# Items of 224 rows, and the start and tail of the work on other queues, in a sigmoid attention with top-1 experts

## The chip, the cores and the metric

The kernel runs on one core of a Trainium2 chip. A core has TensorE (PE, with a separate weight-load stream, PEld), VectorE (DVE), ScalarE (ACT), GpSimd (POOL) and SyncE (SP), and 16 DMA engines that serve the queues into which SP, ACT and POOL issue their transfers. The metric is the device time of one execution in microseconds, as the median of several runs.

## The reference

Attention without softmax for 8 batches, 12 heads, 448 rows and heads of 64, and then for each of the 3584 tokens the one expert of eight that a gate chooses:

```python
def _attn_ref(q, k, v):
    S = q.shape[2]
    scale = 1.0 / np.sqrt(q.shape[-1])
    scores = scale * np.matmul(q, k.transpose(0, 1, 3, 2)) - np.log(S)
    attn = 1.0 / (1.0 + np.exp(-scores))
    return np.matmul(attn, v)

def _moe_ref(x, w_gate, w1, w2):          # x: 3584 x 768
    logits = x @ w_gate                   # 8 experts
    expert_idx = np.argmax(logits, axis=1)
    ...                                   # gate_w: the chosen expert's softmax weight
    for e in range(E):
        mask = expert_idx == e
        h = np.maximum(x[mask] @ w1[e], 0.0)      # 768 -> 1024
        out[mask] = gate_w[mask, None] * (h @ w2[e])   # 1024 -> 768
    return out
```

Everything is float32.

## The kernel before

**Attention.** Two heads make a pair (48 pairs), two pairs a unit (24 units), and a unit takes 7 steps, one for each 64 of the 448 key rows; 168 steps in all. A step makes the scores of two pairs (L541, PE), takes the sigmoid of each (L528, ACT: two activations a step, `at`) and multiplies by the values (L555, PE), which are added up over the 7 steps in PSUM. In the first units the products with the values run two steps behind the scores. The scores have four PSUM buffers, which is two steps: the scores of step 6 are written where those of step 4 stood, after ACT has read them. The order on each engine is the order in which the instructions are written.

For a pair g, k and q are loaded in four DMAs each (`kn`, `qn`, L458; called kg and qg here: k4 is k of pair 4), turned by DVE (L512, `kt`, `qt`), and the values are loaded as `vn`: one DMA for an even pair (L466), two for an odd one (L504). Pairs 0 and 1 are loaded in natural order (`first`, on SP and ACT) and turned by PE. k goes on SP's queue, q on SP's, or on POOL's for pairs 3, 7, 9 and 11. The values of pair 0 go on ACT's queue, those of the pairs up to 15 on POOL's. Within a unit, `READY` says after which step the next loads and turns are written.

SP's and ACT's DMAs share a ring of eight completion counters, called DMAHW0 to DMAHW7 in the order listing, POOL's DMAs have DMASW0 to DMASW7. A DMA that takes a counter in use waits on the issuing engine until the DMA before it on that counter has landed.

**Experts.** When a unit's sums are complete, they are split into a high half (`xh`, L563, a cast on ACT) and a low half (`xl`, L564, DVE), and three products stand for one float32 product. For each batch, all 448 tokens go through the expert that most of them chose (L220 and L239), in between the attention steps from step 36 on. The tokens that chose another expert are recorded in a table in DRAM, `recs`, which is first filled with blank records (L112 to L117), and are computed anew at the end.

**The left-over rows.** At the end the records are cut into items of TL = 256 rows of one expert. A full item goes through `Item.run`: it gathers its rows in two tiles of 128, turns them (L808), multiplies by w1 (stage 1, L869: 144 matmuls with a moving side of TL columns) and by w2 (stage 2, L889: 144 with a stationary side of 128 rows and a moving side of 256 columns), and scatters the two tiles into the output (L818, POOL). An item of at most 32 rows goes another way (`few_first`, `few_turn`, `few_rows`), whose last products run behind the full item's (L929), are scaled by DVE (L933), and are scattered by POOL (L934). With the inputs that are timed there are 218 left-over rows of one expert and one row of another, so one item is full and one has few rows, before the change and after it. A helper, `apart`, tells the framework that two scatters write different rows, so that the second needn't wait for the first; before the change the two scatters of one item are told apart, and those of the few rows are not told apart from them.

Of the kernel before, what the change touches and what calls it, by code (L numbers as in the profile page):

```python
# [19 lines left out]
P = 128  # L20
# [5 lines left out]
def tile_sigmoid_attention_top1_moe(  # L26
# [85 lines left out]
    def blank_records():  # L112
        blank = wpool.tile([P, 1024], U32, tag="wst", bufs=RAWS_AHEAD, name="blank")
        blank3 = blank[:, : E * NT // P * 2].rearrange("p (r w) -> p r w", w=2)
        for w, val in enumerate((int(BIG), 0)):
            nc.gpsimd.iota(blank3[:, :, w], pattern=[[0, E * NT // P]], base=val, channel_multiplier=0)
        nc.gpsimd.dma_start(recs.rearrange("(p r) w -> p r w", p=P), blank3)  # L117
# [376 lines left out]
    def load_values(g):  # L494
        if g >= NG:
            return
        b, hp = divmod(g, NP)
        eng = nc.scalar if g == 0 else nc.gpsimd if g < V_POOL else nc.sync
        t = apool.tile([P, KC, D], F32, tag="vn", bufs=4, name=f"vn_{g}")
        if g % 2 == 0:  # L500
            both_heads(t.rearrange("p c d -> p (c d)"), v, g, eng)
        else:
            for h in range(2):
                eng.dma_start(t[quarter(g, h)], v[b, 2 * hp + h].rearrange("(p c) d -> p c d", c=KC))  # L504
        ops[g, "v"] = t
# [39 lines left out]
    def weighted(s):  # L545
        u, c = divmod(s, ST)
        two = [2 * u + n for n in range(2)]
        for g in two:
            if c == 0:
                pool, tag = (ps_av, "av") if u % 2 == 0 or s >= ALONE else (ps_moe, "moe")  # L550
                psv[g] = pool.tile([P, 512], F32, tag=tag, name=f"av_{g}")
            at = ats.pop((g, c))
            for h in range(2):
                rows = quarter(g, h)
                nc.tensor.matmul(  # L555
                    psv[g][OWN[h], :S], ops[g, "v"][rows, c, :], at[rows], start=(c == 0), stop=(c == KC - 1)
                )
        if c == KC - 1:
            for g in two:
                pv = psv.pop(g)  # L560
                xh = xpool.tile([P, S], F32R, tag="xh", name=f"xh_{g}")
                xl = xpool.tile([P, S], F32R, tag="xl", name=f"xl_{g}")
                nc.scalar.copy(xh, pv[:, :S])  # L563
                nc.vector.tensor_sub(xl, pv[:, :S], xh.bitcast(F32))  # L564
                token_block(g, pv[:, :S])
                xch[divmod(g, NP)] = (xh, xl)

    WARM, V_POOL = 32, 16
# [14 lines left out]
    def attention():  # L583
# [13 lines left out]
        for g in (2, 3):  # L597
            load_values(g)
        blank_records()
# [20 lines left out]
        for s in range(N_ST + 11):  # L620
# [5 lines left out]
            if s < ALONE:  # L626
                steps(s, 1, s - 1)
            elif s == ALONE:
                steps(s, 1, s)
            elif i == ST - 1:  # L630
                steps(s - ST + 2, ST, s + 1)
            yield s, MIX[0]
# [56 lines left out]
    TL = 2 * P  # L689
# [57 lines left out]
    li = rest.tile([1, TL], I32, name="li")  # L747
    nc.vector.tensor_copy(li, pli[0:1, :TL])
    more(8)

    recs_v = recs.rearrange("(i t p) w -> i p t w", t=2, p=P)
    recs_f = recs.rearrange("(i t p) w -> i t p w", t=TL // FEW, p=FEW)
    rec_c = rest.tile([P, 2, 2], U32, name="rec_c")
    rec_n = rest.tile([P, 2, 2], U32, name="rec_n")
# [18 lines left out]
    def load_raw(st, ereg, r):  # L773

        if r < 6:
            f, tp = divmod(r, 3)
            src = w1[bass.ds(ereg, 1), tp * TL : (tp + 1) * TL, f * 512 : (f + 1) * 512]
            nc.sync.dma_start(raw_view(st, 512), src.rearrange("e (t p) f -> p (e t) f", p=P))
        else:
            w2_rows(ereg, r - 6, st)  # L780

    def get_rows(ireg, rec):
        nc.sync.dma_start(rec, recs_v[bass.ds(ireg, 1)].rearrange("o p t w -> (o p) t w"))
        for t in range(2):
            nc.gpsimd.indirect_dma_start(
                out=xg[:, t, :],
                out_offset=None,
                in_=x_tok,
                in_offset=bass.IndirectOffsetOnAxis(ap=rec[:, t, 0:1], axis=0),
                bounds_check=NT - 1,  # L790
                oob_is_err=False,
            )
# [6 lines left out]
    def sort_rows():  # L799
        for t in range(2):  # L800
            sorted_row(xp[:, t], xg[:, t])

    def split_rows(k2):
        px = ps_x.tile([P, 512], F32, tag="px", name=f"px_{k2}")
        for kk in range(2):
            for t in range(2):
                at = kk * TL + t * P
                nc.tensor.transpose(px[:, at : at + P], xp[:, t, 2 * k2 + kk], ident)  # L808
# [6 lines left out]
    def scatter(rec):  # L815
        puts = []
        for t in range(2):
# [3 lines left out]
                in_=xo[:, t, :],  # L821
# [4 lines left out]
            apart(put, puts)  # L826

    pairs, h_two = [], []

    class Item:  # L830
# [23 lines left out]
        def run(self, rec):  # L854
# [25 lines left out]
            for d in range(ND):  # L880
                pss = [ps_m2.tile([P, 512], F32, tag="m2", name=f"ps2_{d}_{h}")[:, :DW] for h in range(2)]
                for n in range(4):
                    whi, wlo = self.part(u)
                    for h in range(2):
                        for i in range(2):
                            hh, hl = (x[:, h * P : (h + 1) * P] for x in hts[2 * n + i])
# [8 lines left out]
                for h in range(2):  # L895
                    to, gate = xo[:, h, d * DW : (d + 1) * DW], rec[:, h, 1:2].bitcast(F32)
# [4 lines left out]
            scatter(rec)  # L901
# [21 lines left out]
    def few_rows():  # L923
# [10 lines left out]
        nc.gpsimd.indirect_dma_start(  # L934
# [6 lines left out]
        )  # L941

# [31 lines left out]
    for t in range(2):  # L974
        nc.gpsimd.indirect_dma_start(
            out=xg[:, t, :],
# [48 lines left out]
    with tc.If(n_items >= 2), tc.manual_schedule():  # L1025
        one.run(rec_c)
    for r in range(9, NR):
        last_raw(r)
    with tc.If(n_few >= 1), tc.manual_schedule():
        few_rows()  # L1030
# [47 lines left out]
```

## Time and profile before

| | |
|---|---|
| median of 3 runs | 824.16 us (823.64 to 824.49) |
| the profiled execution's own time | 823.56 us |
| its span, first to last instruction | 821.5 us |
| PE busy | 810.7 us, 99% |
| DVE, ACT, POOL busy | 398.9, 382.5, 142.9 us |
| mean granted TensorE clock | 0.997 |
| first attention step's scores | 7.8 us after the start |
| stage 1, stage 2 of the full item | 774.8 to 792.0, 792.0 to 809.3 us |
| DMA traffic | 120.68 MB, 147 GB/s |

The lines that the prediction shows come from the page of this execution and from answers of its trace. A row of a timeline has the start and the length in us, the engine, the source line, the operation, its tiles (out<-in) and how many instructions are taken together; in brackets stand the time that the engine sat idle before it and what ended that. SPq, ACTq and POOLq are the queues on which DMAs are issued. A row of the chain that ended last has the start, the length and what it was.

### The profile page before, as it was taken

The page shows a single profiled execution, that of the slowest core. Times are in us where ns is not written, and L with a number is a line of the kernel's source. Part 1 is how long each engine was busy: PE and PEld are TensorE (multiplying, and loading weights), DVE is VectorE, ACT ScalarE, POOL GpSimd, SP SyncE. Part 2 cuts the span into 40 slices and gives each one's busy share as a digit, 9 for nine tenths or more (in the row PEclk, how much of TensorE's full clock was granted, in tenths as well). Part 3 has the DMA queues.
Part 4 walks back from the last instruction along what each step waited for, and adds up shares of the span by engine and source line. Part 5 has one row for each costly group of instructions (what it writes and reads, how often), then busy time and mean ns, then how long its engine had stood idle before and what let it go on. Part 6 is the DMA issues. An engine that isn't in the chain of part 4 may idle for free.

```text
span 821.5 us, 15350 instructions
## 1 busy us (share of the span) xinstructions
PE 810.7 (99%) x5712; PEld 618.2 (75%) x5712; DVE 398.9 (49%) x852; ACT 382.5 (47%) x672; POOL 142.9 (17%) x213
## 2 busy tenths in 40 slices
PE   8999999999999999999999999999999999999995
PEld 5547678677687686786786876876867868999894
DVE  2466346345473264453562544733654435755461
ACT  5865634444525535436344445255362452233250
POOL 4444003110041001310031100410015001512201
PEclk9999999999999999999999999999999999999998
DMA  9999865493485663953847855647635422757840
GB/s 170 162 174 192 216 148 125 108 228 90 116 184 107 163 152 84 204 139 98 184 94 135 203 117 117 165 93 181 127 101 144 127 71 55 204 175 246 273 165 36
DMA packets 287104, 120.68 MB, mean 147 GB/s; under 512 B 200258, under 2 KB 278997, under 8 KB 287024
## 3 DMA queue, kind: packets, MB, share of 16 engines
q1 hardware_dynamic: 277712, 98.81, 51.5%
q0 software_dynamic: 8880, 20.14, 10.3%
q8 instruction: 47, 0.77, 0.4%
q10 hardware_dynamic: 432, 0.69, 0.2%
q14 instruction: 33, 0.27, 0.1%
HBM read 97.55 MB, written 23.17 MB: 147 GB/s over the span
## 4 chain that ended last, share of the span: by engine, by line
PE 98%; DMA 0%; POOL 0%; issue 0%; POOLq 0%; ACT 0%; ACTq 0%
PE ps L239 29%; PE ps L220 29%; PE sc L541 16%; PE av L555 16%; PE psg L267 2%; PE ps L889 2%; PE ps L869 2%; DMA out_dram<-xo,rec_c 0%; PE ps_warm L519 0%; PE pl L276 0%; PE few L912 0%; PE sc_first_k L483 0%; PE sc_first_q L483 0%; PE px L808 0%; PE pg L392 0%
## 5 line engine op out<-in xcount | busy, mean ns | idle before, releaser
L528 ACT ACTIVATE at<-sc,bias_s 128x448 f32<-128x448 f32 x336 | 195.9, 632 | 133.8 <-PE sc L541 132.8
L541 PE MATMUL sc<-qt,kt 64*64 64x448 f32 x1344 | 173.5, 544 | 0.9 <-ACT at L528 0.9
L555 PE MATMUL av<-at,vn 64*64 64x448 f32 x1344 | 172.0, 537 | 0.0
L255 POOL DMA_DIRECT2D out_dram<-ob x96 | 61.4, 651 | 465.7 <-DVE ob L250 387.4
L239 PE MATMUL ps<-hh,w2l 128*128 128x448 f32 x384 | 142.0, 370 | 0.0
L239 PE MATMUL ps<-hh,w2h 128*128 128x448 f32 x384 | 141.6, 369 | 0.0
L220 PE MATMUL ps<-xl,w1h 128*128 128x448 f32 x384 | 141.3, 368 | 0.0
L239 PE MATMUL ps<-hl,w2h 128*128 128x448 f32 x384 | 141.0, 367 | 0.0
L220 PE MATMUL ps<-xh,w1l 128*128 128x448 f32 x384 | 140.6, 366 | 0.0
L220 PE MATMUL ps<-xh,w1h 128*128 128x448 f32 x384 | 140.4, 366 | 0.0
L564 DVE TENSOR_TENSOR xl<-av,xh 128x448 fp32r<-128x448 f32 x48 | 29.1, 605 | 219.8 <-ACT xh L563 217.6
L541 PEld LDWEIGHTS sc<-qt,kt 64*64 64x64 f32 x1344 | 77.4, 189 | 61.6 <-issue 28.1
L225 ACT ACTIVATE hh<-ps 128x448 fp32r<-128x448 f32 x64 | 34.9, 545 | 159.3 <-PE ps L220 159.2
L555 PEld LDWEIGHTS av<-at,vn 64*64 64x64 f32 x1344 | 63.4, 132 | 60.2 <-issue 26.0
L145 ACT CAST w2h<-wst 128x512 fp32r<-128x512 f32 x96 | 61.6, 659 | 86.9 <-PE ps L239 75.3
L220 PEld LDWEIGHTS ps<-xl,w1h 128*128 128x128 f32 x384 | 72.1, 188 | 10.8 <-issue 5.2
L239 PEld LDWEIGHTS ps<-hh,w2h 128*128 128x128 f32 x384 | 72.2, 188 | 9.4 <-issue 4.2
L239 PEld LDWEIGHTS ps<-hh,w2l 128*128 128x128 f32 x384 | 72.2, 188 | 8.3 <-issue 2.8
L220 PEld LDWEIGHTS ps<-xh,w1l 128*128 128x128 f32 x384 | 72.1, 188 | 7.8 <-issue 1.4
L220 PEld LDWEIGHTS ps<-xh,w1h 128*128 128x128 f32 x384 | 72.1, 188 | 6.5 <-issue 0.7
L239 PEld LDWEIGHTS ps<-hl,w2h 128*128 128x128 f32 x384 | 72.2, 188 | 6.0 <-issue 0.4
L146 DVE TENSOR_TENSOR w2l<-wst,w2h 128x512 fp32r<-128x512 f32 x96 | 64.0, 683 | 22.5 <-ACT w2h L145 20.0
(166 smaller groups left out, 737.1 us busy)
## 6 DMA issues: line engine op xcount, KB each, us to landing
wst<-in_moe_w_dram SPq DMA_DIRECT2D x48, 512.0 KB
wst<-in_moe_w_dram SPq DMA_DIRECT2D x56, 384.0 KB
x_tok<-xt SPq DMA_DIRECT2D x64, 168.0 KB
out_dram<-ob POOLq DMA_DIRECT2D x96, 112.0 KB
kn<-in_k_dram SPq DMA_DIRECT2D x184, 56.0 KB
qn<-in_q_dram SPq DMA_DIRECT2D x168, 56.0 KB
raw<-in_moe_w_dram SPq DMA_DIRECT2D x12, 512.0 KB
kept<-in_moe_w_dram SPq DMA_DIRECT2D x12, 512.0 KB
```

The costliest lines, as they stand in the source:

```text
L145: nc.scalar.copy(hi, st)
L146: eng.tensor_tensor(lo, st, hi.bitcast(F32), op=ALU.subtract)
L220: nc.tensor.matmul(ps[:, :S], a[:, ws], b_, start=(t == 0 and n == 0), stop=(t == KD - 1 and n == 2))
L225: nc.scalar.activation(hh[:, :S], ps[:, :S], AF.Relu)
L239: nc.tensor.matmul(ps[:, :S], a, b_, start=(j == 0 and n == 0), stop=(j == KF - 1 and n == 2))
L255: nc.gpsimd.dma_start(out[b * S : (b + 1) * S, cols].rearrange("(j r) f -> r j f", r=32), obv[32 * i : 32 * (i + 1)])
L267: nc.tensor.matmul(psg[: 2 * E, :S], wgs[:, t], xch[b, t][n], start=(t == 0 and n == 0), stop=(t == KD - 1 and n == 1),)
L528: nc.scalar.activation(at, ps[:, :S], AF.Sigmoid, bias=bias_s, scale=SCALE)
L541: nc.tensor.matmul(ps[quarter(g, h), :S], ks, ops[g, "q"][OWN[h]], start=True, stop=True)
L555: nc.tensor.matmul(psv[g][OWN[h], :S], ops[g, "v"][rows, c, :], at[rows], start=(c == 0), stop=(c == KC - 1))
L564: nc.vector.tensor_sub(xl, pv[:, :S], xh.bitcast(F32))
L869: nc.tensor.matmul(pss[j], a[:, js], b_, start=(t == 0 and m == 0), stop=(t == KD - 1 and m == 2))
```

## The change

1. An item has 224 rows in two tiles of 112 (`RT = S // 4`, `TL = 2 * RT`). Stage 1 moves 224 columns, stage 2 has a stationary side of 112, gathers, scatters and transposes have 112 rows, and the tables over the possible items have 128 entries for 112.
2. The scatter of the few rows is told apart from the two of the full item.
3. The values of pairs 2 and 3 are loaded on ACT's queue, after steps 2 and 3 are written, where POOL issued them at the start. The blank records are made where they were, and written by SP after step 12.
4. For units that end before step 35 (five units, ten casts) DVE makes the high half, where ACT did.

```diff
     def blank_records():
         ...
-        nc.gpsimd.dma_start(recs.rearrange("(p r) w -> p r w", p=P), blank3)
+        return lambda: nc.sync.dma_start(recs.rearrange("(p r) w -> p r w", p=P), blank3)
...
     def load_values(g):
...
-        eng = nc.scalar if g == 0 else nc.gpsimd if g < V_POOL else nc.sync
+        eng = nc.scalar if g in V_ACT else nc.gpsimd if g < V_POOL else nc.sync
...
-                nc.scalar.copy(xh, pv[:, :S])
+                if s < ALONE:
+                    nc.vector.tensor_copy(xh, pv[:, :S])
+                else:
+                    nc.scalar.copy(xh, pv[:, :S])
...
-    WARM, V_POOL = 32, 16
+    WARM, V_POOL, V_ACT = 32, 16, (0, 2, 3)
...
-        for g in (2, 3):
-            load_values(g)
-        blank_records()
+        write_blank = blank_records()
         gate_halves()
...
+            if s in (2, 3):
+                load_values(s)
+            elif s == 2 * ST - 2:
+                write_blank()
             yield s, MIX[0]
...
-    TL = 2 * P
+    RT = S // 4
+    TL = 2 * RT
...
     def split_rows(k2):
...
-                at = kk * TL + t * P
-                nc.tensor.transpose(px[:, at : at + P], xp[:, t, 2 * k2 + kk], ident)
+                at = kk * TL + t * RT
+                nc.tensor.transpose(px[:, at : at + RT], xp[:RT, t, 2 * k2 + kk], ident[:RT, :RT])
...
     def scatter(rec):
...
-                in_=xo[:, t, :],
+                in_=xo[:RT, t, :],
...
             apart(put, puts)
+        return puts
...
-                            hh, hl = (x[:, h * P : (h + 1) * P] for x in hts[2 * n + i])
+                            hh, hl = (x[:, h * RT : (h + 1) * RT] for x in hts[2 * n + i])
...
-            scatter(rec)
+            return scatter(rec)
...
-    def few_rows():
+    def few_rows(puts):
...
-        nc.gpsimd.indirect_dma_start(
+        put = nc.gpsimd.indirect_dma_start(
             out=out.rearrange("n (d f) -> (n d) f", d=ND),
...
+        apart(put, puts)
...
-        one.run(rec_c)
+        first_puts = one.run(rec_c)
...
-        few_rows()
+        few_rows(first_puts)
```

How the order on the engines moves, at the two places that matter for the start. A row has the source line, the operation, its tiles with their shape and the counters that it waits for; the number at the end of a tile's name is a buffer number, `at_3` is a sigmoid of step 3, and the ending `_49` stands on every counter.

ScalarE, steps 2 to 4 of the first unit, before:

```order
L528 ACTIVATE at_2_313<-sc_2_307,bias_s 128x448 [waits PE_49]
L528 ACTIVATE at_2_315<-sc_2_308,bias_s 128x448 [waits PE_49]
L528 ACTIVATE at_3_329<-sc_3_323,bias_s 128x448 [waits PE_49]
L528 ACTIVATE at_3_331<-sc_3_324,bias_s 128x448 [waits PE_49]
L528 ACTIVATE at_4_355<-sc_4_349,bias_s 128x448 [waits PE_49,Activation_49]
L528 ACTIVATE at_4_357<-sc_4_350,bias_s 128x448 [waits PE_49,Activation_49]
```

And now:

```order
L529 ACTIVATE at_2_307<-sc_2_301,bias_s 128x448 [waits PE_49]
L529 ACTIVATE at_2_309<-sc_2_302,bias_s 128x448 [waits PE_49]
L467 DMA vn_317<-in_v_dram 128x448 [waits DMAHW4_49]
L529 ACTIVATE at_3_325<-sc_3_319,bias_s 128x448 [waits PE_49]
L529 ACTIVATE at_3_327<-sc_3_320,bias_s 128x448 [waits PE_49]
L505 DMA vn_333<-in_v_dram 64x448 [waits DMAHW3_49]
L505 DMA vn_333<-in_v_dram 64x448 [waits DMAHW5_49]
L529 ACTIVATE at_4_354<-sc_4_348,bias_s 128x448 [waits PE_49,Activation_49]
L529 ACTIVATE at_4_356<-sc_4_349,bias_s 128x448 [waits PE_49,Activation_49]
```

The DMA of values 2 now stands between the sigmoids of steps 2 and 3, the two of values 3 between those of steps 3 and 4, each with a wait for a counter of the ring.

SyncE in the changed kernel, the loads that use these counters (`kn_279` is k4, `qn_284` is q4, `kn_338` is k5; a DMA counts on the counter whose earlier user it waits for):

```order
L459 DMA kn_279<-in_k_dram 32x14x32 [waits DMAHW1_49]
L459 DMA kn_279<-in_k_dram 32x14x32 [waits DMAHW2_49]
L459 DMA kn_279<-in_k_dram 32x14x32 [waits DMAHW3_49]
L459 DMA kn_279<-in_k_dram 32x14x32 [waits DMAHW4_49]
L459 DMA qn_284<-in_q_dram 32x14x32 [waits DMAHW5_49]
L459 DMA qn_284<-in_q_dram 32x14x32 [waits DMAHW6_49]
L459 DMA qn_284<-in_q_dram 32x14x32 [waits DMAHW7_49]
L459 DMA qn_284<-in_q_dram 32x14x32 [waits DMAHW0_49]
L459 DMA kn_338<-in_k_dram 32x14x32 [waits DMAHW1_49]
L459 DMA kn_338<-in_k_dram 32x14x32 [waits DMAHW2_49]
L459 DMA kn_338<-in_k_dram 32x14x32 [waits DMAHW3_49]
L459 DMA kn_338<-in_k_dram 32x14x32 [waits DMAHW5_49]
```

DMAHW4 is taken by k4's fourth DMA and then by values 2, so k5's fourth goes on to DMAHW5; DMAHW3 and DMAHW5 are those of k5's third and fourth DMA, and values 3 take them next. SP's DMAs themselves stand in the same order as before.

On POOL the three DMAs of values 2 and 3 and the write of the blank records are gone from between q3's four DMAs and the split of the gate's weights:

```order
L458 DMA qn_257<-in_q_dram 32x14x32 x4
L466 DMA vn_262<-in_v_dram 128x448
L504 DMA vn_264<-in_v_dram 64x448 [waits DMASW0_49]
L504 DMA vn_264<-in_v_dram 64x448 [waits DMASW1_49]
L116 IOTA blank 128x224 x2
L117 DMA recs<-blank 128x448 [waits DMASW2_49,Pool_49]
L109 CAST wgs<-wg 128x6x8
```

```order
L459 DMA qn_257<-in_q_dram 32x14x32 x4
L117 IOTA blank 128x224 x2
L109 CAST wgs<-wg 128x6x8 [waits DMASW0_49]
```

The split of the gate's weights now carries the wait for the landing of `wg` itself.

More of the change, by code (lines that the diff above doesn't have):

```diff
@@ L746, in tile_sigmoid_attention_top1_moe @@
         nc.tensor.matmul(pli[0:1, a * P : (a + 1) * P], lf[:, a : a + 1], ident, start=True, stop=True)
-    li = rest.tile([1, TL], I32, name="li")
-    nc.vector.tensor_copy(li, pli[0:1, :TL])
+    li = rest.tile([1, 2 * P], I32, name="li")
+    nc.vector.tensor_copy(li, pli[0:1, : 2 * P])
     more(8)
-    recs_v = recs.rearrange("(i t p) w -> i p t w", t=2, p=P)
+    recs_v = recs.rearrange("(i t p) w -> i p t w", t=2, p=RT)
     recs_f = recs.rearrange("(i t p) w -> i t p w", t=TL // FEW, p=FEW)
-    rec_c = rest.tile([P, 2, 2], U32, name="rec_c")
-    rec_n = rest.tile([P, 2, 2], U32, name="rec_n")
+    rec_c = rest.tile([RT, 2, 2], U32, name="rec_c")
+    rec_n = rest.tile([RT, 2, 2], U32, name="rec_n")
     rec_f = rest.tile([ND * FEW, 2], U32, name="rec_f")
@@ L776, in load_raw @@
             f, tp = divmod(r, 3)
-            src = w1[bass.ds(ereg, 1), tp * TL : (tp + 1) * TL, f * 512 : (f + 1) * 512]
+            src = w1[bass.ds(ereg, 1), tp * DW : (tp + 1) * DW, f * 512 : (f + 1) * 512]
             nc.sync.dma_start(raw_view(st, 512), src.rearrange("e (t p) f -> p (e t) f", p=P))
@@ L785, in get_rows @@
             nc.gpsimd.indirect_dma_start(
-                out=xg[:, t, :],
+                out=xg[:RT, t, :],
                 out_offset=None,
@@ L800, in sort_rows @@
         for t in range(2):
-            sorted_row(xp[:, t], xg[:, t])
+            sorted_row(xp[:RT, t], xg[:RT, t])
     def split_rows(k2):
@@ L880, in run @@
             for d in range(ND):
-                pss = [ps_m2.tile([P, 512], F32, tag="m2", name=f"ps2_{d}_{h}")[:, :DW] for h in range(2)]
+                pss = [ps_m2.tile([P, 512], F32, tag="m2", name=f"ps2_{d}_{h}")[:RT, :DW] for h in range(2)]
                 for n in range(4):
@@ L895, in run @@
                 for h in range(2):
-                    to, gate = xo[:, h, d * DW : (d + 1) * DW], rec[:, h, 1:2].bitcast(F32)
+                    to, gate = xo[:RT, h, d * DW : (d + 1) * DW], rec[:, h, 1:2].bitcast(F32)
                     if h == 0:
@@ L975, in tile_sigmoid_attention_top1_moe @@
         nc.gpsimd.indirect_dma_start(
-            out=xg[:, t, :],
+            out=xg[:RT, t, :],
             out_offset=None,
```

## The prediction

> **What bounds the kernel now.** I read the page's table of busy time first, then the chain that ended last (its line by engine), then the windows for the stages that the change touches.
>
> ```profile
> PE 810.7 (99%) x5712; PEld 618.2 (75%) x5712; DVE 398.9 (49%) x852; ACT 382.5 (47%) x672; POOL 142.9 (17%) x213
> PE 98%; DMA 0%; POOL 0%; issue 0%; POOLq 0%; ACT 0%; ACTq 0%
> 7.80:18.00 10.20, 10.20 (x106) 3.87 (x101) 1.70 (x3) 8.81 (x15) 2.85 (x7) 1.00 1.05 165
> 18.00:20.00 2.00, 1.12 (x16) 0.74 (x16) 1.40 (x3) 0.64 (x2) 0.00 (x0) 1.00 0.61 98
> 20.00:44.00 24.00, 24.00 (x260) 14.08 (x256) 9.39 (x17) 21.37 (x38) 9.53 (x16) 1.00 1.06 162
> 52.00:62.00 10.00, 10.00 (x109) 4.67 (x105) 7.33 (x26) 8.50 (x18) 4.31 (x7) 1.00 0.81 166
> ```
>
> A windows row gives the stretch, its length, the busy time of PE, PEld, DVE, ACT and POOL, the granted clock, the DMA engines' share and GB/s. PE is idle for 0.88 us in 18 to 20 and else only in the last 8.6 us. So what comes off ACT, DVE or POOL while PE is full is worth nothing, and what takes PE out of work early on is never won back: from 20 on PE has no gap to close. Three places can move the end: the start, the matmuls of the item, and the tail.
>
> **The start, step by step.** A second view, the timeline of SP, ACT, POOL, DVE and PE up to 24 us (start, length, then the group; in brackets the idle time and what ended it):
>
> ```profile
> 7.13 0.60 POOL L466 DMA_DIRECT2D vn<-in_v_dram  x1
> 8.75 1.05 POOL L504 DMA_DIRECT2D vn<-in_v_dram  x2 [1.02 <-DMA wg<-in_moe_w_gate_dram]
> 9.80 0.70 POOL L116 IOTA blank<- 128x224 uint32 x2
> 10.80 0.57 POOL L117 DMA_DIRECT2D recs<-blank  x1 [0.30 <-POOL blank L116]
> 7.16 9.92 SPq L458 DMA_DIRECT2D kn<-in_k_dram  x8
> 17.13 2.15 SPq L458 DMA_DIRECT2D qn<-in_q_dram  x4
> 19.32 2.05 SPq L458 DMA_DIRECT2D kn<-in_k_dram  x4
> 2.02 0.45 ACTq L466 DMA_DIRECT2D vn<-in_v_dram  x1
> 13.66 1.34 ACT L528 ACTIVATE at<-sc,bias_s 128x448 f32<-128x448 f32 x2 [0.22 <-PE sc L541]
> 15.61 0.54 PE L541 MATMUL sc<-qt,kt 64*64 64x448 f32 x2
> 18.16 0.60 DVE L512 STREAM_TRANSPOSE qt<-qn 128x448 f32<-128x448 f32 x1
> 19.14 0.65 DVE L512 STREAM_TRANSPOSE kt<-kn 128x448 f32<-128x448 f32 x1 [0.38 <-DMA kn<-in_k_dram]
> 18.90 0.65 PE L541 MATMUL sc<-qt,kt 64*64 64x448 f32 x2 [0.88 <-ACT at L528]
> ```
>
> The POOL rows show what a DMA does whose completion counter is still in use: the second values' DMA waits 1.02 us for the landing of an older transfer (wg), and the IOTA written behind it comes after it. The order listing shows the same kind of wait on the changed ScalarE: the DMA of values 2 waits for the counter of the fourth DMA of k4, the two of values 3 for those of the third and fourth DMA of k5, and the sigmoids of steps 3 and 4 stand behind them. (The DMAs numbered k4, q4, k5 are SP's rows from 7.16 on: four of k3 and four of k4, then q4, then k5.) So the question is when the last DMA of k5 lands; call it T.
>
> As now: k4's last DMA is issued by 7.16 + 9.92 = 17.08 and DVE turns it at 19.14, so a landing is at most 2.06 us behind the issue. k5's are issued by 19.32 + 2.05 = 21.37, so T = 23.4 in the kernel before.
>
> In the changed kernel three transfers of 224 KB (values 2, values 3, blank records) are gone from POOL's queue in this stretch. The eight DMAs at 7.16 take 9.92 us where eight at the pace of 19.32 (2.05 for four) take 4.10, and the DMA engines' share is 1.05, so it is the full engines that hold SP. At the 201 GB/s of the first stretch (row below) the three transfers take 3 x 0.229 / 0.201 = 3.4 us. T = 23.4 - 3.4 = 20.0. The lower bound is SP at its free pace from 7.16 on: 16 DMAs x 0.51 = 8.2, plus 2.06, T = 17.4; the upper is no help at all, 23.4. I take 20.0, since 165 and 201 GB/s in the two stretches say that the engines are full.
>
> What T does: the last DMA of values 3 is issued in 0.45 (row at 2.02), a gap of some 0.1 goes with it, so the first sigmoid of step 4 runs from T + 0.55, takes half of 1.34, less overlap, 0.64, and PE's scores of step 6, which reuse its PSUM buffer (four buffers, two a step), start at T + 1.28. Now they start at 15.60 (row 15.61). Delay: T - 14.32 = 5.7. In return the stall of 0.88 us ahead of 18.90 goes: it ends as DVE's turned q3 does (18.16 + 0.60 = 18.76), which is long done when PE comes there late. **Net: T - 14.32 - 0.88 = T - 15.20 = +4.80 us**; between +2.2 (T = 17.4) and +8.2 (T = 23.4). ACT can't give it back, since PE is full from 20 to 44 (24.00 of 24.00). Values 3 themselves, landing some 3 us after T, are wanted at step 9, 4.5 us after step 6, and are in time.
>
> The Trainium skill, "DMA: Bandwidth & Descriptors", section "Anatomy of one DMA — SWDGE (gpsimd) path", says that DMA engines do not wait on semaphores and that any such wait happens on the issuing sequencer before dispatch; by that rule the whole wait lies on ScalarE. The POOL rows above agree with it (1.02 us, with the IOTA behind).
>
> **The item.** Windows, groups and the chain of waits for 740 to 822 (start, us, what):
>
> ```profile
> 0.00:7.80 7.80, 6.52 (x146) 6.42 (x148) 2.73 (x9) 2.02 (x3) 7.05 (x21) 1.00 0.84 201
> 752.21 0.44 PE px L808 x4
> 756.77 9.73 PE ps L239 x48
> 774.79 17.26 PE ps L869 x144
> 792.05 17.29 PE ps L889 x144
> 775.00:792.00 17.00, 17.00 (x144) 17.00 (x143) 11.07 (x19) 9.14 (x19) 2.51 (x4) 1.00 0.88 305
> 792.00:810.00 18.00, 18.00 (x157) 17.59 (x158) 8.01 (x15) 6.64 (x13) 0.60 (x1) 1.00 0.01 2
> ```
>
> Stage 1 (L869) moves 256 columns in 17.26 / 144 = 119.9 ns; L239 moves 448 in 9.73 / 48 = 202.7. The slope is 82.8 / 192 = 0.431 ns a column, so 224 columns give 106.1. The four transposes with 128 moving columns take 0.44 / 4 = 110 each, which speaks for a floor near 110 (another number format, so a weak row). I take 108.5 between them: 144 x 11.4 = **-1.64 us**, between -2.0 (106.1) and nothing (a floor at today's 119.9). No row shows a shorter matmul that is dearer, which excludes a loss. Stage 2 (L889) still moves 256 columns, its stationary side goes from 128 to 112 wide: nothing. ACT and DVE, which feed stage 1, are at 9.1 and 11.1 of 17 us and go on beside it; the DMA share of 0.01 after 792 says that the weights are in by then.
>
> The Trainium skill, "TensorE: Matmul & The Clock Gate", section "LDWEIGHTS (loading the stationary operand)", puts the loading of a stationary side at its columns over 1.2 per ns, 107 ns for 128; by that the pitch could not go below 107 and the gain would be 1.86 at most. The transposes' 110 agrees.
>
> **The tail.** Timeline of the last stretch:
>
> ```profile
> 808.65 0.47 ACT L898 ACTIVATE xo<-ps,rec_c 128x256 f32<-128x256 f32 x1 [5.29 <-PE ps L889]
> 809.40 1.06 POOL L818 DMA_INDIRECT out_dram<-xo,rec_c  x1 [29.99 <-PE ps L889]
> 813.02 0.48 DVE L933 TENSOR_SCALAR few_t<-few,rec_f 96x256 f32<-96x256 f32 x1 [3.17 <-PE few L929]
> 815.15 0.94 POOL L934 DMA_INDIRECT out_dram<-few_t,at_f  x1 [3.37 <-DMA out_dram<-xo,rec_c]
> 810.77 3.44 DMA out_dram<-xo,rec_c
> ```
>
> The few rows' scatter now waits for the item's second scatter (810.77 + 3.44 = 814.21). Without that it waits for DVE alone, done at 813.50. The first scatter starts 0.28 after its ACT producer (809.12 to 809.40), so I put it at 813.78: **-1.37 us**. It could be less: from the landing at 814.21 to the start at 815.15 pass 0.94, and with that the gain is 0.71; without any gain, 0.
>
> **Edits at nothing.** Ten casts move from ACT to DVE up to step 35. DVE is at 9.39 of 24 in 20 to 44 and at 7.33 of 10 in 52 to 62, and the subtraction that follows waits for the cast anyway; if that cover went, the price would be about 0.6 per unit, the length of a DVE copy of that size (the turn at 18.16 takes 0.60). The blank write at step 12 is one SP DMA, 0.5 us between loads that have a unit's time to arrive. Gathers and scatters of 112 rows, tables with 128 entries for 112 and transposes of 112 columns lie where PE works from its own buffers.
>
> **Sum.** 823.56 (the profiled run, 2.06 outside its span of 821.5) + 4.80 - 1.64 - 1.37 = 825.35. The median of the runs is 824.16, 0.60 above the profiled run, so I forecast 825.9, or +0.2%.
>
> **Rivals.**
>
> *ScalarE is not held* (0.17).
>
> ```profile
> 0.85 1.28 ACT L82 ACT_TABLE_LOAD   x1 [0.85 <-PEq L1064]
> 1.13 0.86 ACTq L466 DMA_DIRECT2D first<-in_q_dram  x2
> ```
>
> ACT's queue issues its first DMAs while its table load runs. If the sigmoids likewise go past the waiting DMAs, or these waits end as they are met, only the gains stay: the stall of 0.88 goes too, since k3 is early. 823.56 - 0.88 - 1.64 - 1.37 = 819.67, with the 0.60 820.3: faster. Against it: here a DMA that waits for nothing runs beside work issued before it; no row shows work passing a DMA that waits, and POOL's IOTA did not. With the hold in place the change becomes a gain when the net at the start is under 3.01, at T below 18.2, which the free pace (17.4) only just allows.
>
> *SP gets no faster* (0.07). Its queue is held by the landings in its own ring rather than by the three transfers, T = 23.4, the start costs 8.2 and the sum is 823.56 + 8.20 - 3.01 + 0.60 = 829.4.
>
> *The clock falls* (0.11). The two waits leave PE idle twice, some 2.5 us before step 5's scores and 2.5 before step 6's.
>
> ```profile
> 814.00:816.00 2.00, 0.00 (x0) 0.00 (x0) 0.00 (x0) 0.00 (x0) 0.85 (x1) 1.00 0.01 4
> 816.00:818.00 2.00, 0.00 (x0) 0.00 (x0) 0.00 (x0) 0.00 (x0) 0.09 (x1) 0.60 0.05 10
> ```
>
> The last matmul ends at 812.9, the clock is whole up to 816 and halved a bit later, some 3.5 us after it. Gaps of 2.5 are shorter; if it falls all the same and takes as long to come back, half of 3.5 is lost: +1.7, 827.6. The Trainium skill, "TensorE: Matmul & The Clock Gate", "Part 1: The HAM clock gate", has a window of about 3.4 us that runs free of the kernel, so that one idle window halves the clock; the row agrees with 3.5.
>
> *The item and the tail don't do what they say* (0.03). Pitch stays at 119.9 and the scatter still waits: 823.56 + 4.80 + 0.60 = 829.0.
>
> **How the numbers follow.** The forecast case has 0.62; with T of 18.5 to 21.5 its own range is 824.4 to 827.4. What a measurement can tell from no change is 0.2%, 1.65 us: faster is below 822.5, slower above 825.8. The forecast stands on that edge: 0.33 of its 0.62 is slower, 0.28 the same and 0.01 faster. Faster: 0.17 + 0.01 = 0.18. Slower: 0.33 + 0.07 + 0.11 + 0.03 = 0.54. Same: 0.28. The range, 823.0 to 828.8, leaves out the case in which ScalarE is not held and the two at 829 and above.
>
> **What would show it.** In the changed profile: ACT's rows of the values' DMAs at about 16 and 20 us, and the sigmoids of steps 3 and 4 behind them; PE idle twice between 14 and 21.5, and the stall at 18.90 gone; step 6's scores at 21.3; L869's 144 in 15.3 to 15.8; few's scatter 0.3 after DVE's last row. The forecast is wrong if sigmoids run from 13.7 on as now, or if SP's DMAs of k5 land before 18.

## The result, and the profile after

| | before | changed |
|---|---|---|
| median | 824.16 us (5 runs, 823.13 to 824.49) | 828.25 us (5 runs, 828.05 to 830.04) |
| ratio | | 1.0057, 95% interval 1.0043 to 1.0072 |
| the profiled execution's own time and span | 823.56, 821.5 us | 830.04, 828.4 us |
| mean granted clock | 0.997 | 0.994 |

The change makes the kernel slower by 4.1 us, on the side that the prediction gave 0.54, but more than the 1.8 us that it forecast. The profiled execution is the slowest of the five.

The page of the changed kernel, its busy times and the engines of the chain that ended last:

```profile
PE 813.8 (98%) x5712; PEld 623.0 (75%) x5712; DVE 404.6 (49%) x862; ACT 376.6 (45%) x662; POOL 139.6 (17%) x209
PE 96%; DMA 1%; SPq 1%; issue 1%; POOL 0%; ACTq 0%; POOLq 0%; ACT 0%
```

PE is busy 3 us longer with the same 5712 matmuls, and the chain now holds SP's queue and DMAs. The windows of the start show both (length, then the busy times of PE, PEld, DVE, ACT and POOL, the granted clock, the DMA share, GB/s):

```profile
7.80:18.00 10.20, 8.21 (x104) 3.50 (x100) 3.08 (x5) 4.68 (x10) 0.51 (x3) 1.00 0.89 119
18.00:20.00 2.00, 2.00 (x16) 0.75 (x16) 0.00 (x0) 0.42 (x1) 0.00 (x0) 1.00 0.97 217
20.00:22.00 2.00, 0.19 (x2) 0.00 (x0) 0.00 (x0) 0.00 (x0) 0.00 (x0) 1.00 0.78 95
22.00:24.00 2.00, 0.00 (x0) 0.00 (x0) 0.00 (x0) 0.15 (x1) 0.00 (x0) 0.81 0.56 90
24.00:26.00 2.00, 1.47 (x8) 0.94 (x12) 0.00 (x0) 2.00 (x4) 0.00 (x0) 0.50 1.02 203
26.00:28.00 2.00, 2.00 (x16) 1.22 (x12) 0.65 (x1) 1.21 (x3) 0.00 (x0) 0.50 0.73 116
28.00:32.00 4.00, 4.00 (x36) 2.74 (x32) 0.00 (x0) 1.81 (x4) 0.00 (x0) 0.74 0.76 154
```

PE is idle for 2 us before 18 and for over 4 us in 20 to 24.5, where before the change it lost 0.88 us; then it works at half clock until some way into 28 to 32. The timelines of ACT and PE name the two waits:

```profile
10.55 2.73 ACT L529 ACTIVATE at<-sc,bias_s 128x448 f32<-128x448 f32 x5 [0.21 <-PE sc L542]
16.88 0.33 ACTq L467 DMA_DIRECT2D vn<-in_v_dram  x1
17.26 1.16 ACT L529 ACTIVATE at<-sc,bias_s 128x448 f32<-128x448 f32 x2 [3.98 <-DMA kn<-in_k_dram]
22.58 1.16 ACTq L505 DMA_DIRECT2D vn<-in_v_dram  x2
23.85 2.21 ACT L529 ACTIVATE at<-sc,bias_s 128x448 f32<-128x448 f32 x4 [5.43 <-issue]
17.95 1.12 PE L542 MATMUL sc<-qt,kt 64*64 64x448 f32 x6 [1.99 <-ACT at L529]
24.53 2.28 PE L542 MATMUL sc<-qt,kt 64*64 64x448 f32 x8 [4.34 <-ACT at L529]
```

The sigmoids of step 3 wait 3.98 us for the landing of a k, though their scores have long been there: the DMA of values 2 is written ahead of them, and it is issued at 16.88, when k4's last DMA has landed (16.86 by the trace's landing events). The sigmoids of step 4 start at 23.85, behind the two DMAs of values 3. The first of these waits for k5's third DMA, which lands at 22.55 by the landing events, and is issued from 22.58 to 23.10; k5's last DMA, for which the second waits, lands meanwhile, at 22.74, and the second is issued from 23.14 to 23.74. In the second of these rows the idle time is put down to "issue", since what ScalarE was waiting on is its own DMA in front.

The item, from the chain that ended last (start, us, what), and the tail's timeline:

```profile
784.91 16.07 PE ps L877 x144
800.98 16.85 PE ps L897 x144
821.51 0.48 DVE L941 TENSOR_SCALAR few_t<-few,rec_f 96x256 f32<-96x256 f32 x1 [3.17 <-PE few L937]
822.27 0.92 POOL L942 DMA_INDIRECT out_dram<-few_t,at_f  x1 [2.07 <-DVE few_t L941]
```

Stage 1 went from 17.26 to 16.07 us, stage 2 from 17.29 to 16.85, and the few rows' scatter starts 0.28 after VectorE's last row ends (821.99 to 822.27), as forecast. These gains are there; the start took more.

The profiled execution's 6.48 us add up so. Step 10's first scores come at 33.33 instead of 22.73: +10.60, of which 8.05 is the hold on step 6's scores (24.53 - 15.60 - 0.88) and the rest, 2.55, goes with the half clock behind it (PE works at half clock from 24.53 to some 30 us). From there to stage 1 it wins 0.48 back, stage 1 gives -1.19, stage 2 -0.44, the tail from the end of stage 2 on -1.59, and outside the span 1.64 us pass for 2.06 (-0.42). 10.60 - 0.48 - 1.19 - 0.44 - 1.59 - 0.42 = 6.48.

### The profile page after: what moved, and what is told of

It is laid out like the page before. It is cut to its first block, busy times and chain, and to the rows that moved or that the text cites. A ratio compares the mean times of both kernels' runs of the same rounds, so it can differ in the third digit from the quotient of the medians.

```text
span 828.4 us, 15349 instructions
## 1 busy us (share of the span) xinstructions
PE 813.8 (98%) x5712; PEld 623.0 (75%) x5712; DVE 404.6 (49%) x862; ACT 376.6 (45%) x662; POOL 139.6 (17%) x209
## 4 chain that ended last, share of the span: by engine, by line
PE 96%; DMA 1%; SPq 1%; issue 1%; POOL 0%; ACTq 0%; POOLq 0%; ACT 0%
PE ps L240 29%; PE ps L221 29%; PE sc L542 16%; PE av L556 15%; PE psg L268 2%; PE ps L897 2%; PE ps L877 2%; DMA kn<-in_k_dram 1%; SPq L459 1%; PE pl L277 0%; PE few L920 0%; PE pg L393 0%; PE px L815 0%; ACTq L505 0%; SPq L467 0%
## 5 line engine op out<-in xcount | busy, mean ns | idle before, releaser
L542 PE MATMUL sc<-qt,kt 64*64 64x448 f32 x1344 | 169.1, 549 | 6.3 <-ACT at L529 6.3
L556 PE MATMUL av<-at,vn 64*64 64x448 f32 x1344 | 166.7, 540 | 0.0
L542 PEld LDWEIGHTS sc<-qt,kt 64*64 64x64 f32 x1344 | 74.7, 189 | 65.6 <-issue 25.3
```

The costliest lines, as they stand in the source:

```text
L542: nc.tensor.matmul(ps[quarter(g, h), :S], ks, ops[g, "q"][OWN[h]], start=True, stop=True)
L556: nc.tensor.matmul(psv[g][OWN[h], :S], ops[g, "v"][rows, c, :], at[rows], start=(c == 0), stop=(c == KC - 1))
```

## The experiments

Theory: ScalarE's DMAs wait for late landings ahead of sigmoids (the hold), and the idle PE then loses its clock. Rivals: the values come late; DMAs on ScalarE cost as such; the blank write or the casts cost; the clock plays no part. The kernels were timed in four sets, each beside runs of the kernel before, so that the ratios compare across sets and the microseconds only within one.

| kernel | median, us | before, us | ratio (95%) |
|---|---|---|---|
| changed kernel, again (two runs) | 827.82 | 823.16 | 1.0056 (1.0039 to 1.0074) |
| values on POOL, late | 820.04 | 823.16 | 0.9963 (0.9950 to 0.9976) |
| values on POOL, at the start | 820.80 | 823.16 | 0.9976 (0.9964 to 0.9988) |
| fillers in the second gap | 827.09 | 823.16 | 1.0044 (1.0031 to 1.0057) |
| 224 rows alone | 822.20 | 822.94 | 0.9993 (0.9984 to 1.0002) |
| scatter told apart, alone | 821.87 | 822.94 | 0.9987 (0.9978 to 0.9996) |
| casts alone | 822.62 | 822.94 | 0.9997 (0.9988 to 1.0006) |
| values late and blank records on POOL | 819.97 | 822.94 | 0.9965 (0.9951 to 0.9979) |
| only values 3 on ScalarE | 830.01 | 823.91 | 1.0077 (1.0063 to 1.0091) |
| only values 2 on ScalarE | 825.39 | 823.91 | 1.0014 (1.0005 to 1.0023) |
| values on ScalarE, at the start | 821.07 | 823.91 | 0.9964 (0.9951 to 0.9978) |
| half the columns in stage 1 | 829.55 (one run) | 823.91 | |
| changed kernel, once more | 829.44 | 823.17 | 1.0074 (1.0060 to 1.0088) |
| fillers in both gaps | 827.31 | 823.17 | 1.0051 (1.0037 to 1.0064) |
| values on SP | 820.71 | 823.17 | 0.9969 (0.9957 to 0.9981) |

### The changed kernel again

No edit.

> The changed kernel once more, for a second profile. The first one was taken of an execution of 830.0 us, 1.8 above the median of 828.25: its first scores came 0.95 us later than before (8.73 against 7.78), k5's last DMA landed at 22.7, PE waited 4.3 us for step 6 and the clock was at 0.50 from about 23 to 30. If the hold on ScalarE and the clock are the cause, every execution shows both waits; I expect first scores near 7.8 again, the landing of k5 between 20 and 22, PE idle 2.5 to 4 us ahead of step 6, and the clock down for some 3 us within 20 to 30. If the 0.95 at the start belongs to the change, it is there again.

PE's rows at the two gaps:

```profile
17.94 1.12 PE L542 MATMUL sc<-qt,kt 64*64 64x448 f32 x6 [1.60 <-ACT at L529]
24.39 2.28 PE L542 MATMUL sc<-qt,kt 64*64 64x448 f32 x8 [4.20 <-ACT at L529]
```

Both waits are there, k5 lands at 22.59, the clock is at 0.52 and 0.63 in 24 to 28. The first scores come at 9.11, even later than in the first profile, but over all runs of this study they lie between 7.8 and 9.2 whatever the kernel (7.83 in the next one): this lateness isn't the change's. It also doesn't count here: step 6 waits for a landing, and starts at 24.4 in an execution that began at 9.11 as in one that began at 8.73.

### Who issues the values

```diff
-    WARM, V_POOL, V_ACT = 32, 16, (0, 2, 3)
+    WARM, V_POOL, V_ACT = 32, 16, (0,)
```

> The changed kernel with values 2 and 3 issued at the same places in the program (after steps 2 and 3) but by POOL in place of ScalarE; the blank records are still written by SP at step 12. Hold theory (ScalarE's sigmoids stand behind the DMAs' waits): POOL has nothing behind these DMAs that PE waits for, so both PE gaps go and the clock stays, 820 to 821.5 us. Rival (it is the late loading of the values, or the order of the loads on the DMA engines): the loss stays, 826 to 829.

820.04 us: 7.8 us under the changed kernel in the same set, and 3.1 under the kernel before. The timelines of ACT and PE:

```profile
13.71 1.34 ACT L529 ACTIVATE at<-sc,bias_s 128x448 f32<-128x448 f32 x2 [0.22 <-PE sc L542]
18.49 0.65 PE L542 MATMUL sc<-qt,kt 64*64 64x448 f32 x2 [0.41 <-DVE qt L513]
```

The sigmoids of step 4 run at 13.71, as before the change (13.66), and of the old stall of 0.88 us 0.41 is left, now with its right name, the turned q of pair 3. The values' places in the program are the same, only the engine differs, and with ScalarE free of these DMAs the loss is gone: the hold is shown. Late values are not tested by this run, since POOL issues them at 9.04 to 10.15 here, where ScalarE issued them at 16.88 and 22.58. But the waits of PE in the changed kernel from 16 to 60 us (total, times, longest) name sigmoids alone and no values:

```profile
PE sc L542 <- ACT at L529: 6.3, 2, 4.3
```

> The changed kernel with values 2 and 3 on POOL at the start, as before the change; only the blank records stay late and on SP. Hold theory: no wait on ScalarE, 820 to 821.5 us (the item's and the tail's gains of 1.6 and 1.6, and what is won of the old stall of 0.88 by the blank records' absence). Rival (the blank write on SP at step 12, or the casts on VectorE, cost something): 823 or more.

Here the three DMAs of the values go back to POOL's queue at the start as well, in the same edit of `V_ACT` and with the two calls of `load_values` put back ahead of the blank records. 820.80: no hold, though its twelve runs spread wider than those of any other kernel here (819.29 to 824.02). PE is full through 18 to 44, but it waits at another place. The waits of PE and the timeline of DVE, 44 us on:

```profile
PE pl L277 <- DVE g L272: 1.8, 1, 1.8
50.92 0.65 DVE L513 STREAM_TRANSPOSE kt<-kn 128x448 f32<-128x448 f32 x1 [4.32 <-DMA kn<-in_k_dram]
51.49 0.57 DVE L272 COPY g<-psg 16x448 f32<-16x448 f32 x1
```

The gate's transposes wait for a DVE copy that stands behind the turn of a k that landed late. So here PE runs into SP's loads at 50 us. The eight DMAs of k in question are issued from 43.49 on, where the kernel before issues them from 40.54; why they come later is not shown.

### ScalarE as issuer, without the wait

```diff
         load_values(1)
+        for g in (2, 3):
+            load_values(g)
         warm_up(WARM)
...
-            if s in (2, 3):
-                load_values(s)
-            elif s == 2 * ST - 2:
+            if s == 2 * ST - 2:
```

> The changed kernel with values 2 and 3 on ScalarE's queue, but issued at the start, right behind values 0, where the ring's counters are free (two of the three DMAs wait for early loads that land by 5 to 7 us). Hold theory: it isn't ScalarE as issuer that costs, but the wait for a late landing in front of sigmoids. No gap at steps 5 and 6, 820 to 821.5; the turned q of pair 0 may be up to 1 us late. Rival (DMAs issued by ScalarE cost whatever their place): 824 or more.

Ratio 0.9964. The same three DMAs on the same engine cost nothing at a place where the counters that they take are free early: what costs is the landing that they wait for.

### Each of the two waits

```diff
-    WARM, V_POOL, V_ACT = 32, 16, (0, 2, 3)
+    WARM, V_POOL, V_ACT = 32, 16, (0, 3)
```

> The changed kernel with only values 3 issued by ScalarE (after step 3), values 2 by POOL at their late place. Theory A (each wait ends at a landing, a fixed time, so the later one alone sets the loss and the first is swallowed by it): k5's last DMA lands at about 22 to 23, step 6's scores begin 1.8 us later at about 24 to 24.5, PE is idle in one piece of 5 us or more, the clock falls, and the time is that of the changed kernel, 827 to 829. Theory B (the two waits add up, or values 2's transfer in front of k5's delays it): the time is clearly under that, 823 to 826, with the landing of k5 near 21.

```diff
-    WARM, V_POOL, V_ACT = 32, 16, (0, 2, 3)
+    WARM, V_POOL, V_ACT = 32, 16, (0, 2)
```

> The changed kernel with only values 2 issued by ScalarE (after step 2), values 3 by POOL at their late place. Theory A: only the first wait is left; k4's last DMA lands near 16.9, step 5's scores begin near 18 instead of 14.1, 3.9 us later, of which 0.4 to 0.9 was stall anyway, and no clock is lost in a gap of 2 to 3.4 us: 820.0 + 3.2 = 823.2. If the first wait were swallowed by other work: 820 to 821.

PE's gap in the one with values 3 alone, and then in the one with values 2 alone:

```profile
24.09 1.76 PE L542 MATMUL sc<-qt,kt 64*64 64x448 f32 x6 [7.51 <-ACT at L529]
```

```profile
18.80 1.12 PE L542 MATMUL sc<-qt,kt 64*64 64x448 f32 x6 [2.66 <-ACT at L529]
```

With values 3 alone, step 6 starts at 24.09, as with both (24.39 to 24.53), and the ratio is 1.0077: the later wait alone makes the whole loss, and the earlier one is swallowed by it. That is theory A, and it costs no less for being one wait: PE is idle in one piece of 7.51 us, and the clock was at 0.50 already in 22 to 24. (The second DMA of values 3 takes another counter there, that of q5's first DMA, which lands at 22.80.) With values 2 alone the loss against the kernel with none on ScalarE is 0.0051 (1.0014 - 0.9963), 4.2 us, more than the 3.2 expected. The eleven runs of this kernel point to the clock for the difference: five took 823.92 to 824.44 us at a mean clock of 0.998, six took 825.39 to 826.27 at 0.996. The first five lie 3.3 us above the kernel with none on ScalarE, as expected, and the others 1.6 more, about the price of a fallen clock; the profile is one of the first five, so the fall itself was not traced.

This pair also corrects a step of the prediction. k5's last DMA lands at 22.54 with values 2 on POOL, where its issue ended at 20.48 (2.06 us before, just the figure taken), and at 22.74 with values 2 on ScalarE, where its issue ended at 19.14, 3.6 us before: there the transfer of values 2, issued at 16.88, lies in front of k5's, issued from 17.10 on. But the landing itself is only 0.2 us later there. Values 2 on POOL are issued at 9.67, ahead of k4, and k5 lands at 22.54 all the same, where the prediction had 20.0 and theory B 21. With values 2 alone on ScalarE k5 lands at 23.65, and with none there at 22.91. So, by one profile each, the place of values 2 makes 0.2 to 0.7 us of T, and not the 2.7 by which T was missed.

### The clock

```diff
+            if s in (5, 6):
+                warm_up({5: 22, 6: 60}[s])
             if s < ALONE:
                 steps(s, 1, s - 1)
```

A first trial had 40 fillers ahead of step 6 alone.

> The changed kernel with 40 matmuls of ones (128 columns, results unused, some 2.2 us at full clock) on PE ahead of the scores of step 6, in the gap in which PE waits for ScalarE. The fillers take no work away and leave the hold as it is. If the fallen clock is part of the loss: PE's longest idle time drops below the 3.5 us at which the clock fell at the end of the kernel before, the clock stays at 1.00 in 20 to 30 and the time falls by 1.5 to 3 us, to 825.5 to 826.7. If the loss is the hold alone: unchanged at 828.2, or longer where the fillers outlast the gap.

827.09, only 0.7 under the changed kernel of that set. The windows show why:

```profile
16.00:18.00 2.00, 0.41 (x2) 0.19 (x4) 0.00 (x0) 1.10 (x2) 0.00 (x0) 0.94 0.64 104
18.00:20.00 2.00, 2.00 (x14) 0.95 (x12) 0.00 (x0) 0.06 (x1) 0.00 (x0) 0.50 1.05 224
20.00:22.00 2.00, 2.00 (x19) 0.74 (x14) 0.00 (x0) 0.00 (x0) 0.00 (x0) 0.71 0.60 95
```

In this execution the clock fell after the first gap already, which was 2.54 us long. So fillers were put into both gaps, and the changed kernel was run beside them.

> The changed kernel once more, timed beside the next two on one chip: 1.005 to 1.0057 of the kernel before, with the clock down for 3 to 7 us between 22 and 30.

> The changed kernel with unused matmuls of ones on PE in both gaps: 22 ahead of step 5's scores (some 1.3 us) and 60 ahead of step 6's (some 3.6 us). The hold is left as it is; step 6's scores begin near 24.3 as before. If the clock is part of the loss: it stays at 1.00 from 8 to 32 us and the time is 1.5 to 3 us under that of the changed kernel on the same chip. If the hold alone is the loss: no difference (within 0.3 us).

The windows of the changed kernel in this set, and then of the one with both fillers:

```profile
18.00:20.00 2.00, 1.99 (x14) 1.00 (x16) 0.00 (x0) 0.48 (x1) 0.00 (x0) 0.73 0.90 206
20.00:22.00 2.00, 1.44 (x6) 0.00 (x0) 0.00 (x0) 0.00 (x0) 0.00 (x0) 0.50 0.74 108
24.00:26.00 2.00, 1.49 (x8) 0.96 (x12) 0.00 (x0) 2.00 (x4) 0.00 (x0) 0.50 1.00 200
26.00:28.00 2.00, 2.00 (x16) 1.21 (x12) 0.65 (x1) 1.19 (x3) 0.00 (x0) 0.50 0.76 121
28.00:32.00 4.00, 4.00 (x40) 2.85 (x36) 0.42 (x1) 2.27 (x4) 0.16 (x1) 0.85 0.74 152
```

```profile
18.00:20.00 2.00, 1.23 (x12) 0.67 (x14) 0.00 (x0) 1.16 (x2) 0.00 (x0) 1.00 0.87 183
20.00:22.00 2.00, 2.00 (x29) 1.20 (x22) 0.00 (x0) 0.00 (x0) 0.00 (x0) 1.00 0.98 152
24.00:26.00 2.00, 2.00 (x23) 1.25 (x24) 0.54 (x1) 2.00 (x5) 0.00 (x0) 1.00 1.07 216
26.00:28.00 2.00, 2.00 (x26) 1.71 (x22) 0.11 (x1) 1.99 (x4) 0.00 (x0) 1.00 0.75 121
28.00:32.00 4.00, 4.00 (x48) 3.29 (x44) 2.71 (x5) 2.97 (x6) 2.45 (x4) 1.00 0.57 100
```

Step 6's scores start at 24.52 and 24.45, so the hold is the same; the clock is whole with the fillers, step 10 starts at 30.51 instead of 32.87, and the median is 827.31 instead of 829.44, 2.1 us less. The intervals of the two ratios overlap by 0.0004, but all five runs with fillers (826.06 to 828.42) lie under all five without (828.55 to 829.58). The clock's part of the loss is shown: some 2 us. The hold's part is the rest. How far the clock falls differs from one execution of the changed kernel to the next (mean clock 0.992 to 0.996).

### The other parts, each alone

224 rows alone (the change's edits of `TL`, `RT`, the tiles and the tables, nothing else):

> The kernel before with the items of 224 rows in two tiles of 112 alone; start, tail and casts as they were. In the changed kernel's profile stage 1 took 16.07 for 17.26 us and stage 2 16.85 for 17.29. If that is due to the rows alone, the time falls by 1.6 us (0.2%) and both stages show the same lengths. Rival of the prediction (only stage 1 gains, 1.64): stage 2 stays at 17.29.

The chain that ended last in this kernel:

```profile
775.99 16.07 PE ps L872 x144
792.06 16.85 PE ps L892 x144
810.30 4.03 DMA out_dram<-xo,rec_c
```

Both stages have the new lengths, 1.63 us less together, but the time falls by 0.7 (interval from -1.3 to +0.2). One part of the missing 0.9 stands in the last row: the item's second scatter takes 4.03 us to land instead of 3.44, and here the few rows' scatter still waits for it, so 0.6 us are given back there. By the landing events it takes 4.03 to 4.04 in three kernels with 112 rows a tile and 3.44 to 3.54 in three with 128. The rest is within the interval.

The scatter told apart, alone:

```diff
-        nc.gpsimd.indirect_dma_start(
+        put = nc.gpsimd.indirect_dma_start(
             out=out.rearrange("n (d f) -> (n d) f", d=ND),
...
+        apart(put, puts)
```

> The kernel before with the few rows' scatter told apart from the item's two scatters, and nothing else. Forecast of the prediction: the few rows' scatter starts 0.28 us after VectorE's last row instead of 0.94 after the landing, 1.37 us earlier, and the time falls by 1.4 (0.17%). If the later landing of the item's second scatter sets the end instead, nothing is gained.

```profile
813.92 0.48 DVE L934 TENSOR_SCALAR few_t<-few,rec_f 96x256 f32<-96x256 f32 x1 [3.17 <-PE few L930]
814.68 0.94 POOL L935 DMA_INDIRECT out_dram<-few_t,at_f  x1 [1.99 <-DVE few_t L934]
```

814.40 to 814.68: 0.28, and -1.1 us in the median (-1.8 to -0.3), with 1.4 forecast. Besides, it makes the two changes more than a sum: with it the landing that grew to 4.03 isn't waited for.

Ten casts on VectorE, alone:

> The kernel before with the ten casts of the high halves on VectorE, and nothing else. Forecast of the prediction: no change (within 0.3 us), since PE is full from 20 us on. Rival, from the two kernels above in which PE waits 0.4 and 1.8 us at the gate's transposes near 50 us for VectorE: the casts make VectorE late there, and PE shows such a wait, 0.5 to 2 us.

-0.3 us, no change that can be told, and no wait at the gate's transposes. The rival falls as far as the casts alone go.

### The blank records, and a best version

```diff
-        return lambda: nc.sync.dma_start(recs.rearrange("(p r) w -> p r w", p=P), blank3)
+        return lambda: nc.gpsimd.dma_start(recs.rearrange("(p r) w -> p r w", p=P), blank3)
...
-    WARM, V_POOL, V_ACT = 32, 16, (0, 2, 3)
+    WARM, V_POOL, V_ACT = 32, 16, (0,)
```

> The changed kernel with values 2 and 3 on POOL at the late places, and the blank records also written by POOL, after step 12. SP is spared one DMA of 0.4 us between loads. In the kernel that differs from it only by the blank write on SP, PE waited 0.35 us near 50 us for VectorE, which waited for a late load of SP's. If SP's queue is what makes that load late: no wait there, 819.7, 0.4 less than 820.04. If the wait is the casts' doing: it stays, 820.0.

819.97 us, 0.9965, and no wait at 50 us. But this execution's first scores came at 9.24 where the other's came at 7.83, so that PE was less far ahead there; and the median is the same. What the blank write on SP costs can't be told from this.

```diff
-        eng = nc.scalar if g in V_ACT else nc.gpsimd if g < V_POOL else nc.sync
+        eng = nc.scalar if g in V_ACT else nc.sync if g in (2, 3) else nc.gpsimd if g < V_POOL else nc.sync
```

with values 2 and 3 written right behind the loads of pairs 2 and 3, `V_ACT` without 2 and 3 and the blank records on POOL:

> The changed kernel with values 2 and 3 on SP's queue right behind k3, blank records on POOL. SP has no work behind its DMAs that PE waits for at once, and k3 is ahead of the values on the DMA engines, so the stall ahead of step 7's second scores (0.2 to 0.9 us) may go: 819.5 to 820 in the terms of the first chip (ratio 0.995 to 0.9965). If SP's own pace sets the later loads, its three more DMAs make k and q late between 40 and 52 us and PE waits there: ratio 0.9965 to 0.998.

0.9969: the stall at step 7 is gone, and PE waits 0.46 us at the gate's transposes near 50 us. It is no better. The versions without a held ScalarE all lie at 0.9963 to 0.9976; the plainest of them, the change with values 2 and 3 issued by POOL at the same places, is 3.1 us faster than the kernel before and 7.8 faster than the changed one.

### Stage 1's pitch

```diff
-                                pss[j], a[:, js], b_, start=(t == 0 and m == 0), ...
+                                pss[j][:, :RT], a[:, js], b_[:, :RT], start=(t == 0 and m == 0), ...
```

and the halves of `hh` and `hl` both made from these columns, so that the kernel leaves out the products of the item's other 112 rows.

> The kernel with values 2, 3 and blank records on POOL at the late places and casts on ScalarE; stage 1 of the item computes only the first 112 of 224 rows (the other half is filled with a copy of it, so half of the item's rows are wrong). It measures stage 1's pitch at 112 moving columns beside 119.0 ns at 256 and 110.8 at 224 (first to last start over 144). If the pitch goes by columns with the slope of 256 to 448 (0.43 ns a column): about 60 to 70 ns, 9 to 10 us for the stage. If the 128 stationary columns set a floor: 105 to 111 ns, 15.1 to 16.0 us.

From the chain, and then from the windows of this kernel:

```profile
775.69 3.86 PE ps L874 x35
785.28 13.69 PE ps L874 x63
780.00:790.00 10.00, 9.61 (x64) 9.34 (x64) 5.88 (x14) 4.81 (x14) 0.32 (x1) 0.75 1.08 369
790.00:800.00 10.00, 10.00 (x49) 10.00 (x49) 3.52 (x10) 3.37 (x10) 0.00 (x0) 0.50 0.03 12
```

At whole clock 35 matmuls with 112 columns take 3.86 us, 110.3 ns each, hardly less than the 111.6 with 224 columns (16.07 / 144). So there is a floor near 110 ns that the moving columns don't set, and 224 columns already lie on it. The stationary side is the same 128 columns in both, and the transposes that moved 128 columns had 110 as well. The weight loads (PEld) are busy for all of 790 to 800. That the loading of the stationary side is the floor agrees with that, and with the rule of the Trainium skill, "TensorE: Matmul & The Clock Gate", section "LDWEIGHTS (loading the stationary operand)", which gives 107; a run with a narrower stationary side in stage 1 was not made. The stage as a whole took longer (23 us), because the clock fell to 0.50.

## Why the prediction was right or wrong

- **ScalarE is held: right**, and its two places too. It had 0.62 together with the term's size, and with the two cases that only move that size (clock, SP's pace) 0.80. The rival that it isn't held fell.
- **The size of the hold: wrong, in the step "T = 23.4 - 3.4 = 20.0".** In the kernel before, k5's last DMA landed at 23.38, as worked out. In the changed kernel it landed at 22.74 (22.59 to 22.74 in its three profiles), so the three transfers' absence was worth 0.65 us and not 3.4, and T was near the upper bound of 23.4. Part of the error is a miscount: one of the three, values 2, only moved and is still ahead of k5. But two transfers at 3.4 / 3 each would still give T = 21.1. The rows of the DMA queues up to T (queue, kind, packets, MB, share of the 16 engines' time; q1 is SP's queue, q0 POOL's, q10 ACT's) show the rest, first those of the kernel before (0 to 23.38 us), then those of the changed one (0 to 22.74):

```profile
q1 hardware_dynamic: 11888, 1.89, 53.2%
q0 software_dynamic: 493, 1.24, 28.1%
q10 hardware_dynamic: 432, 0.69, 8.1%
```

```profile
q1 hardware_dynamic: 12574, 1.98, 57.8%
q0 software_dynamic: 256, 0.48, 14.9%
q10 hardware_dynamic: 576, 0.92, 12.2%
```

On the mean of the 16 engines POOL's packets took 6.57 us up to T before (28.1% of 23.38) and 3.39 after, so 3.2 us were freed, near the 3.4 forecast. But ACT's packets took 0.9 more (values 2), SP's own 0.7 more, and for 0.95 more the engines had no packet. What the step had wrong is to turn freed transfer time into an earlier landing one for one; why SP's loads did not move up into it stays open.
- **From T to step 6's scores: 1.28 forecast, 1.79 measured** (22.74 to 24.53). The forecast put one issue of 0.45 and a gap behind T. Two issues stood behind the landing of k5's third DMA at 22.55, and they took 1.16 us beside SP's. The net at the start was 8.05 and not 4.80.
- **The clock: wrong in its chance.** The gaps were put at 2.5 us each, under the 3.5 after which the clock had fallen at the end of the kernel before, so the case got 0.11. The second gap was 3.07 to 4.34 us long in the three profiles of the changed kernel, since T was late, and the clock fell in all of them, for about 2 us of the loss; in one of them, and in the trial with fillers in the second gap alone, it fell after a first gap of 2.5 us already. The 3.5 was the wrong yardstick, as the last section shows. The price named, 1.7, was about right.
- **Stage 1: 1.64 forecast, 1.19 measured.** The step is the 108.5 taken between 106.1 and 110; it is 111.6, on the floor. **Stage 2: nothing forecast, 0.44 gained**: the narrower stationary side took its pitch from 120.1 to 117.0 ns with the same 256 moving columns. The item as a whole gained 1.63, by two errors that cancel.
- **The tail: right.** The scatter starts 0.28 after VectorE; alone 1.1 us by the median against 1.4.
- **Edits at nothing: right for the casts alone.** In three of the five kernels with the casts on VectorE and no held ScalarE, PE met a wait of 0.35 to 1.8 us near 50 us at SP's loads, which the sum had not seen; the changed kernel shows no such wait.
- With the measured terms of its own profile the forecast's sum would be 823.56 + 8.05 + 2.55 - 1.63 - 1.59 = 830.9, beside 830.04. Among the forecast's cases, that is T near 23.4 (0.07) and the fallen clock (0.11) together, which none of them had. That the median, 828.25, still lies in the range given is luck in part: 0.9 us of gains between the stages and outside the span, which no term names, offset some of the loss.

## What to carry to other kernels

A DMA put on an engine that also computes brings its waits with it: look which counter it takes, whose transfer used that last, when this lands, and what stands behind it on that engine; the same DMA was free at a place where its counter was free. Count a moved transfer in the queue that it moves into, and don't take the time of the transfers that go away for an earlier landing of those that stay: here 3.2 us freed gave 0.65. And price an idle TensorE by its gap and by the clock behind it: here a hold of some 8 us cost 2 more.

## What the runs showed of the hardware that was not expected

- The granted clock fell after PE had been idle for 2.46 and 2.54 us between busy stretches (to 0.50 in the windows behind), and did not fall after gaps of 1.60, 1.99, 2.39 and 2.66 us. The Trainium skill, "TensorE: Matmul & The Clock Gate", "Part 1: The HAM clock gate", has a window of 3.4 us that runs free of the kernel; a gap that starts anywhere in it agrees with a fall after some gaps and not after others, but not with a wholly idle window in 2.5 us. The traces' records of the granted clock show what decides. In each execution the clock changes only at times that lie whole multiples of 3.41 us apart; in the three profiles of the changed kernel it was halved for 6.83, 3.41 and 10.24 us. Cut into windows of 3.41 us on these times, the first falls came at the end of windows in which PE had been busy for 0.37, 0.00 and 0.95 us (the changed kernel), 0.87 (fillers in the second gap alone) and 0.00 (values 3 alone). Windows with 1.43 us (behind the gap of 2.66, which lies across two of them) and with 1.88, 2.03 and 2.24 us kept the whole clock. So between 0.95 and 1.43 us of work in such a window made the difference here, and a gap of 2.46 us that lies in one window cost the clock where 2.66 did not.
- The clock also fell with PE hardly ever idle: with 112 columns per matmul at 110.3 ns, 1.0 column a ns, it went to a mean of 0.75 in 780 to 790 and to 0.50 in 790 to 800, with PE busy for 19.61 of these 20 us, where stage 1 with 224 columns at 111.6 ns, 2.0 a ns, kept 1.00. That the columns per ns are the cause is argued from this one pair of kernels.
- A narrower stationary side (112 for 128 columns) made matmuls with the same 256 moving columns faster, 117.0 for 120.1 ns.
